# Three of four MLP batches by a seven-product scheme with weight sums kept in DRAM

## The chip, the cores and the metric

The kernel runs on one core of one Trainium2 chip. The metric is the device time of one execution in microseconds (us). Before the change three runs took 1020.67, 1022.09 and 1023.76 us; the median is 1022.09 us.

The core has a matrix engine (TensorE, PE in the profile; its weight loads are listed as PEld), a vector engine (VectorE, DVE), a scalar engine (ScalarE, ACT), GpSimd (POOL), and SyncE (SP), which here only issues DMAs. Matmuls write to PSUM, a memory of eight banks of 128 x 512 float32; GpSimd works on SBUF, the main on-chip memory. Each engine works through its own queue in order. A DMA waits, on the queue that issues it, for what it needs.

## What is computed

```python
def _attn_ref(q, k, v, centroids):          # B, H, S, D = 4, 8, 768, 64
    # q and k rows are assigned to one of 16 clusters each; a query sees the keys of its own cluster
    ...
    attn = softmax(where(mask, scale * q @ k.T, -1e9))
    return attn @ v

def _moe_ref(x, U, V, w_ch1, w_ch2):        # x: 4 x 768 x 512, w_ch1: 512 x 2048, w_ch2: 2048 x 512
    h = x.transpose(0, 2, 1) @ U @ V        # rank 32
    u = x + h.transpose(0, 2, 1)
    ch = np.maximum(u @ w_ch1, 0.0) @ w_ch2
    return u + ch
```

The change is in the last two lines, the MLP: two products with a ReLU between them, in four batches of 768 rows. All is float32.

## The kernel before

**Precision.** The MLP's products are done in a reduced 32-bit matmul type (F32R). A float32 value is therefore split into a high part (ScalarE copies it to F32R) and a low part (VectorE or GpSimd subtracts the high part). A product is three matmuls: high x high, high x low, low x high.

**Weights.** w1 and w2 arrive as the bits of 64-bit numbers, in four groups g of 512 hidden columns, each in 8 pieces of 128 x 512 (4 of w1, 4 of w2). `load_weights` takes a piece through six stages: a DMA (L151), ScalarE (`upper`, L159), three VectorE steps on integers (`join`, L171 to L183), and the split: ScalarE copies the high part (L204), GpSimd or VectorE subtracts (L205). The result stays in SBUF as `wg[g]` = w1h, w1l, w2h, w2l. Groups 0 and 1 are ready before the MLP begins, groups 2 and 3 are still being joined during its first half batch.

**The MLP.** There are eight half batches i of 384 rows. `fetch_u` reads the rows from DRAM, `turn_u` transposes them on PE (12 transposes) and splits them. Then come 16 steps f, one for each 128 hidden columns: `gemm1` (L606 to L608) makes 12 matmuls of 384 columns into one bank, ScalarE takes the ReLU as hh (L611), VectorE the low part hl (L612); `gemm2` (L622 to L624) uses hh and hl as stationary operands in 9 matmuls of 512 columns, which accumulate in three banks over all 16 steps. `gemm2` of step f comes after `gemm1` of step f + 1. `finish` adds u (L630) and stores 128 x 512 blocks.

**The order of work** is a list of events with planned times in units of one step f. The MLP begins at M0, half batch i at M0 + 16 i. The list is sorted by time, and each engine's instructions are fixed in that order; the times themselves are only a sort key. What runs late on an engine delays all that stands behind it there.

Of the kernel before, what the change touches and what calls it, by code (L numbers as in the profile page):

```python
# [52 lines left out]
FG = NF // NG  # L53
# [64 lines left out]
def clustered_attention_moe(ctx: ExitStack, tc: tile.TileContext, qk, v, cen, moe_U, moe_V, w1, w2, out):  # L118
# [68 lines left out]
    parts, pool = {}, {}  # L187
# [33 lines left out]
    def in_arena(at, k, n):  # L221
        return arena[:, at:at + k * n].rearrange("p (k n) -> p k n", k=k)
# [101 lines left out]
    n = B * NP  # L324
    NS = 2 * NT
    NG4 = 4 * NT
    live = {}
# [237 lines left out]
            nc.sync.dma_start(out=u_scr[b], in_=x)  # L565


    nh = 2 * B

    free = 2 * XS + 4 * 2048  # L570
    turned = {0: [in_arena(free, ND, HS), in_arena(free + ND * HS, ND, HS)]}

    def open_mlp():

        early.close()
        sb = pool["sb"] = ctx.enter_context(tc.tile_pool(name="msb", bufs=1, reuse_waits="tile"))
        pool["y"] = ctx.enter_context(tc.tile_pool(name="ps_y", bufs=4, space=PSUM, reuse_waits="tile"))
        wg[2].append(weight_tile(2, "w2l", sb))
        turned[1] = [sb.tile([P, ND, HS], F32R, name=name) for name in ("uh", "ul")]

    def open_weights():
        tail.close()
        right = ctx.enter_context(tc.tile_pool(name="wpool3", bufs=1, side="right", reuse_waits="tile"))
        wg[3] = [weight_tile(3, name, right) for name in names]

    def fetch_u(i):
# [13 lines left out]
    def gemm1(i, f):  # L600
        w1h, w1l, _, _ = wg[f // FG]
        uh, ul = turned[i % 2]
        fs = slice((f % FG) * P, (f % FG) * P + P)
        ps = work("ps_h")
        for d in range(ND):
            nc.tensor.matmul(ps[:, 0:HS], w1h[:, d, fs], uh[:, d, :], start=(d == 0), stop=False)  # L606
            nc.tensor.matmul(ps[:, 0:HS], w1h[:, d, fs], ul[:, d, :], start=False, stop=False)  # L607
            nc.tensor.matmul(ps[:, 0:HS], w1l[:, d, fs], uh[:, d, :], start=False, stop=(d == ND - 1))  # L608
        hh = pool["sb"].tile([P, HS], F32R, name="hh", bufs=3)
        hl = pool["sb"].tile([P, HS], F32R, name="hl", bufs=3)  # L610
        nc.scalar.activation(hh, ps[:, 0:HS], AF.Relu)  # L611
        nc.vector.scalar_tensor_tensor(out=hl, in0=ps[:, 0:HS], scalar=0.0, in1=hh, op0=ALU.max, op1=ALU.subtract)  # L612
        live["h", i, f] = hh, hl
# [12 lines left out]
    def finish(i):  # L626
        b, h = divmod(i, 2)
        u, y = live.pop(("u", i)), live.pop(("y", i))
        for t in range(HT):
            nc.vector.tensor_add(u[:, t, :], y[t], u[:, t, :])  # L630
            nc.sync.dma_start(out=out[b, (h * HT + t) * P:(h * HT + t + 1) * P, :], in_=u[:, t, :])

# [35 lines left out]
    for i in range(n):  # L668
# [24 lines left out]
        for k in range(NS):  # L693
            h, c = divmod(k, NT)
# [10 lines left out]
    for b, (t_u, t_sum, t_v) in enumerate(zip(*mixes.values())):  # L705
        o = NS * (NP * b + NP - 1)
# [58 lines left out]
```

## Time and profile before

| | |
|---|---|
| runs | 1020.67, 1022.09, 1023.76 us |
| profiled execution: span from first to last instruction | 1018.5 us |
| its own time beside the span | not given; the median of the runs is 3.6 us above the span |
| MLP: first gemm1 matmul to the last gemm2 matmul | 463.1 to 1014.2 us |
| one steady half batch | 68.3 us |
| granted PE clock in the MLP | 1.00 |

The profile is one execution. A group row gives the line of the code, the engine, the operation, output and inputs, shape and count, then the sum of busy time and the mean length, then the idle time before it and what ended it. In an order-of-time view the first number is the start, the second the length. A busy PE need not be at its peak: matmuls are pipelined, so the distance from start to start is their price, and it is shorter than the length shown.

### The profile page before, as it was taken

The page shows a single profiled execution, that of the slowest core. Times are in us where ns is not written, and L with a number is a line of the kernel's source. Part 1 is how long each engine was busy: PE and PEld are TensorE (multiplying, and loading weights), DVE is VectorE, ACT ScalarE, POOL GpSimd, SP SyncE. Part 2 cuts the span into 40 slices and gives each one's busy share as a digit, 9 for nine tenths or more (in the row PEclk, how much of TensorE's full clock was granted, in tenths as well). Part 3 has the DMA queues.
Part 4 walks back from the last instruction along what each step waited for, and adds up shares of the span by engine and source line. Part 5 has one row for each costly group of instructions (what it writes and reads, how often), then busy time and mean ns, then how long its engine had stood idle before and what let it go on. Part 6 is the DMA issues. An engine that isn't in the chain of part 4 may idle for free.

```text
span 1018.5 us, 13723 instructions
## 1 busy us (share of the span) xinstructions
PE 990.5 (97%) x5368; PEld 786.9 (77%) x5368; DVE 490.5 (48%) x914; ACT 347.7 (34%) x572; POOL 359.4 (35%) x246
## 2 busy tenths in 40 slices
PE   5899999999999999989999999999999999999998
PEld 3566666676667666657899999999999999998997
DVE  5797777777777666768772121121221211212211
ACT  4454554555556554564341111111111111111110
POOL 5466676888788967753230000000000000000000
PEclk9899999999999999999999999999999999999999
DMA  7754554656465636243431001010010010100000
GB/s 186 191 130 115 157 146 122 192 155 156 100 199 136 150 86 181 61 143 108 163 123 63 1 32 32 1 62 1 1 63 1 18 46 1 62 1 1 32 1 32
DMA packets 28687, 87.71 MB, mean 86 GB/s; under 512 B 4880, under 2 KB 9488, under 8 KB 28112
## 3 DMA queue, kind: packets, MB, share of 16 engines
q1 hardware_dynamic: 28240, 86.76, 30.5%
q8 instruction: 42, 0.69, 0.3%
q14 instruction: 21, 0.17, 0.1%
q10 hardware_dynamic: 384, 0.10, 0.0%
HBM read 42.99 MB, written 12.58 MB: 55 GB/s over the span
## 4 chain that ended last, share of the span: by engine, by line
PE 90%; DVE 5%; ACT 1%; issue 1%; POOL 1%; DMA 1%; ACTq 0%; SPq 0%; POOLq 0%; DVEq 0%
PE o_ps L500 12%; PE ps_h L606 9%; PE ps_h L608 9%; PE ps_h L607 9%; PE y L624 9%; PE y L623 9%; PE y L622 9%; PE ps_max L453 7%; PE st L477 6%; PE st L479 6%; DVE m L455 2%; PE ps_sum L512 1%; PE ps_sim L343 1%; PE ps_oT L533 1%; PE ps_uT L595 1%
## 5 line engine op out<-in xcount | busy, mean ns | idle before, releaser
L492 POOL TENSOR_TENSOR T<-T,pr 128x768 f32<-128x768 f32 x120 | 226.5, 1887 | 44.9 <-ACT pr L482 19.3
L612 DVE SCALAR_TENSOR_TENSOR hl<-ps_h,hh 128x384 fp32r<-128x384 f32 x128 | 71.2, 556 | 349.9 <-ACT hh L611 349.8
L455 DVE TENSOR_REDUCE m<-ps_max 128x1 f32<-128x384 f32 x384 | 195.2, 547 | 80.6 <-PE ps_max L453 79.0
L611 ACT ACTIVATE hh<-ps_h 128x384 fp32r<-128x384 f32 x128 | 62.9, 491 | 373.8 <-PE ps_h L608 373.8
L482 ACT ACTIVATE pr<-st 128x768 f32<-128x768 f32 x192 | 154.3, 812 | 83.5 <-PE st L479 65.4
L453 PE MATMUL ps_max<-arena 128*128 128x384 f32 x384 | 126.6, 380 | 6.9 <-DVE oh L369 2.5
L500 PE MATMUL o_ps<-pr,vt 128*64 128x384 f32 x768 | 132.2, 494 | 0.1
L623 PE MATMUL y<-w2l,hh 128*128 128x512 f32 x288 | 113.6, 395 | 0.0
L477 PE MATMUL st<-arena 128*128 128x384 f32 x384 | 104.9, 354 | 2.0 <-ACT pr L482 2.0
L453 PEld LDWEIGHTS ps_max<-arena 128*128 128x128 f32 x384 | 70.5, 192 | 45.4 <-issue 21.4
L500 PEld LDWEIGHTS o_ps<-pr,vt 128*64 128x64 f32 x768 | 52.7, 138 | 66.4 <-issue 59.8
L479 PE MATMUL st<-arena 97*128 97x384 f32 x384 | 99.2, 340 | 2.8 <-DMA arena<-mT 2.8
L477 PEld LDWEIGHTS st<-arena 128*128 128x128 f32 x384 | 66.2, 190 | 17.9 <-issue 9.3
L492 POOL TENSOR_TENSOR T<-pr 128x768 f32<-128x768 f32 x30 | 56.6, 1886 | 62.2 <-ACT pr L482 62.2
L624 PE MATMUL y<-w2h,hl 128*128 128x512 f32 x192 | 76.1, 396 | 0.0
L624 PE MATMUL y<-arena,hl 128*128 128x512 f32 x192 | 76.0, 396 | 0.0
L622 PE MATMUL y<-w2h,hh 128*128 128x512 f32 x192 | 75.1, 391 | 0.0
L622 PE MATMUL y<-arena,hh 128*128 128x512 f32 x192 | 74.8, 390 | 0.0
L479 PEld LDWEIGHTS st<-arena 97*128 97x128 f32 x384 | 70.4, 190 | 3.5 <-issue 2.2
L623 PEld LDWEIGHTS y<-w2l,hh 128*128 128x128 f32 x288 | 54.0, 188 | 9.1
L504 ACT COPY os<-o_ps 128x384 f32<-128x384 f32 x32 | 15.3, 480 | 104.7 <-PE o_ps L500 104.7
L606 PE MATMUL ps_h<-arena,w1h 128*128 128x384 f32 x128 | 44.8, 350 | 0.2 <-DVE arena L598 0.2
(132 smaller groups left out, 1597.3 us busy)
## 6 DMA issues: line engine op xcount, KB each, us to landing
rw<-in_w SPq DMA_DIRECT2D x32, 512.0 KB
R<-in_qk SPq DMA_DIRECT2D x32, 384.0 KB
arena<-arena SPq DMA_DIRECT2D x32, 384.0 KB
arena<-arena SPq DMA_DIRECT2D x64, 192.0 KB
vt<-in_v SPq DMA_DIRECT2D x16, 384.0 KB
u_scr<-xt SPq DMA_DIRECT2D x4, 1536.0 KB
u<-u_scr SPq DMA_DIRECT2D x8, 768.0 KB
out_y<-u SPq DMA_DIRECT2D x24, 256.0 KB
```

The source lines that it names most:

```text
L453: nc.tensor.matmul(ps[:, 0:HS], x1[:, 0, g // 2, g % 2, t * P:(t + 1) * P], x1[:, 1, h, g % 2, :], start=True, stop=True)
L455: nc.vector.reduce_max(live["m2", i][:, h, u:u + 1], ps[:, 0:HS], axis=AX.X)
L477: nc.tensor.matmul(st[:, j, 0:HS], x1[:, 1, hk, j, ks], x1[:, 0, h, j, :], start=True, stop=False)
L479: nc.tensor.matmul(st[:, j, 0:HS], x2[0:97, 1, hk, j, ks], x2[0:97, 0, h, j, :], start=False, stop=True)
L482: nc.scalar.activation(pr, st[:, :, 0:HS], AF.Exp, scale=SCALE)
L492: eng.tensor_add(T, live["p", i, h, 0] if c == 1 else T, live["p", i, h, c])
L500: nc.tensor.matmul(o_ps[64 * j:64 * j + 64, 0:HS], vv[:, c, j, :], pr[:, j, :], start=(c == 0), stop=(c == NT - 1))
L606: nc.tensor.matmul(ps[:, 0:HS], w1h[:, d, fs], uh[:, d, :], start=(d == 0), stop=False)
L607: nc.tensor.matmul(ps[:, 0:HS], w1h[:, d, fs], ul[:, d, :], start=False, stop=False)
L622: nc.tensor.matmul(y[t], hh[:, ts], w2h[:, f % FG, :], start=(f == 0), stop=False)
L623: nc.tensor.matmul(y[t], hh[:, ts], w2l[:, f % FG, :], start=False, stop=False)
L624: nc.tensor.matmul(y[t], hl[:, ts], w2h[:, f % FG, :], start=False, stop=(f == NF - 1))
```

## The change

Batch 0 (half batches i = 0 and 1, `nh = 2`) stays as it was. Batches 1 to 3 go another way: each product of a 2 x 2 block matrix is made by seven block products in place of eight (Strassen's scheme in Winograd's form).

**Sums of weights.** For each of the four groups and for w1 and w2, the four 256 x 256 blocks A11, A12, A21, A22 give four sums S1 to S4. This is done once, during batch 0: `recover` adds high and low parts (VectorE, 4 a step), `combine` makes the sums (GpSimd, 4), `split` splits them again (ScalarE copy, GpSimd subtract, then a DMA; 4, in two output buffers that take turns), `store_block` writes A11, A12, A22 (6 DMAs). Seven high and low blocks of a step, 3.67 MB, go to DRAM (`wc`); eight steps, one every 2.9 f-steps from M0 + 1 on.

**Batches 1 to 3.** `fetch_half` and `turn_half` bring in u as before, transposed; `u_sums` (VectorE) and `u_halves` (ScalarE, GpSimd) make its seven split blocks. A batch is 16 stretches of seven products: eight of the first matrix (`seven1`, K = 0 to 7) and eight of the second (`seven2`), in the order 1 1 1 2 1 2 1 2 1 2 1 2 1 2 2 2. A product is 6 matmuls of 384 columns with the weights stationary, into a PSUM bank of its own; the eight banks go round. So the output is transposed, and the host turns it back. `after1` adds the products up in SBUF (VectorE; ReLU on ScalarE), `h_sums` (VectorE) and `h_halves` (ScalarE, GpSimd) make the seven split blocks of the hidden layer, `after2` adds the second products to y and to four accumulators, `join_up` joins these after a batch; in the last batch `after2` does so itself in its last two stretches. The weights come from `wc` by `fetch_w1` and `fetch_w2`, two buffers deep, 29.4 MB a batch, all on SP's queue.

The rest moves buffers and reads w1 in another row order. The diff, cut:

```diff
+    wc = [[dram.tile([P, 2, 7, 512], F32, name=f"wc{k}_{g}") for g in range(NG)] for k in range(2)]
...
-    nh = 2 * B
+    nh = 2
...
+    def store_block(k, g, name, part):
+        nc.sync.dma_start(out=wc[k][g][:, :, slot[k][name], part * 256:part * 256 + 256],
+                          in_=blocks(k, g, part)[name].bitcast(F32))
+    def recover(k, g, j):
+        hi, lo = (blocks(k, g, part)[("A21", "A11", "A22", "A12")[j]] for part in range(2))
+        nc.vector.tensor_add(temps(k)[j], hi.bitcast(F32), lo.bitcast(F32))
+    def combine(k, j):
+        f = temps(k)
+        if j == 0:
+            nc.gpsimd.tensor_sub(f[1], f[0], f[1])
...
+    def split(k, g, j):
+        w = temps(k)[(1, 0, 2, 3)[j]]
+        o = pool["f"][:, 4096 + 1024 * (j % 2):5120 + 1024 * (j % 2)].rearrange("p (a n) -> p a n", a=2)
+        hi, lo = (o[:, :, part * 256:part * 256 + 256] for part in range(2))
+        nc.scalar.copy(hi.bitcast(F32R), w)
+        nc.gpsimd.tensor_sub(lo.bitcast(F32R), w, hi)
+        nc.sync.dma_start(out=wc[k][g][:, :, slot[k][("S3", "S1", "S2", "S4")[j]], :], in_=o)
...
+    def bank():
+        count["bank"] += 1
+        ps = work("ps_p") if count["bank"] % 2 else pool["y"].tile([P, 512], F32, name="ps_q", tag="y")
+        return ps[:, 0:HS]
...
+    def seven1(b, K, s):
+        ps = live["p", b, K, order[0][s]] = bank()
+        w = w1s[K % 2][:, 512 * s:512 * s + 512].rearrange("p (h k q) -> p h k q", h=2, k=2)
+        u = uc[order[0][s]]
+        for k in range(2):
+            nc.tensor.matmul(ps, w[:, 0, k], u[:, 0, k], start=(k == 0), stop=False)
+            nc.tensor.matmul(ps, w[:, 0, k], u[:, 1, k], start=False, stop=False)
+            nc.tensor.matmul(ps, w[:, 1, k], u[:, 0, k], start=False, stop=(k == 1))
...
+        elif key == T1:
+            h[B22] = ring()
+            add(h[B22], ps, h[B21])
+            add(h[B12], ps, h[B12])
+            nc.scalar.activation(h[B22], h[B22], AF.Relu)
...
+    def h_halves(b, K, key):
+        x = live["f", b, K][key]
+        out_ = live["h", b, K, key] = spare.pop(0)
+        hi, lo = out_[:, 0], out_[:, 1]
+        nc.scalar.copy(hi, x)
+        nc.gpsimd.tensor_sub(lo, x, hi)
...
+    def after2(b, m, e):
+        s, q = divmod(e, 2)
+        key = order[1][s]
+        ps = live.pop(("q", b, m, e))
+        y = pool["ys"][b % 2]
+        own = {B22: y[:, q, 1], B21: y[:, q, 0], T4: y[:, q + 2, 0]}.get(key)
+        if own is None:
+            own = pool["acc"][key][:, q]
+            if m == 0:
+                nc.scalar.copy(own, ps)
+                return
+        nc.vector.tensor_add(own, ps, own)
+        if b < B - 1 or m < NG - 1:
+            return
...
+    for k, (g, j) in enumerate((g, j) for g in range(NG) for j in range(2)):
+        c = M0 + 1 + 2.9 * k
+        for r in range(4):
+            at(c + 0.3 * r, recover, j, g, r)
+            at(c + 0.9 + 0.6 * r, combine, j, r)
+            at(c + 1.2 + 0.6 * r, split, j, g, r)
+        for r, name in enumerate(("A11", "A12", "A22")):
+            for half in range(2):
+                at(c + 0.4 * (2 * r + half), store_block, j, g, name, half)
...
+    U = 0.25
+    for b in range(1, B):
+        o = M0 + NF * nh + 28 * (b - 1)
...
+        seq = [(1, 0), (1, 1), (1, 2), (2, 0), (1, 3), (2, 1), (1, 4), (2, 2), (1, 5), (2, 3),
+               (1, 6), (2, 4), (1, 7), (2, 5), (2, 6), (2, 7)]
...
-        "in_w1": bits["w1"].reshape(ND, P, NG, FG * P).transpose(2, 1, 0, 3),
+        "in_w1": bits["w1"].reshape(ND, P, NG, FG, P).transpose(2, 1, 3, 0, 4).reshape(NG, P, FG, ND * P),
...
-    return r.results[0]["out_y"]
+    y = r.results[0]["out_y"].reshape(B, S, DM)
+    return np.concatenate([y[:1], y[1:].reshape(B - 1, DM, S).transpose(0, 2, 1)])
```

More of the change, by code (lines that the diff above doesn't have):

```diff
@@ new lines, in clustered_attention_moe, with blocks @@
+    order = ((B11, T2, T3, T1, B21, T4, B22), (B22, B11, B21, T1, T3, T2, T4))
+    slot = [{left[key]: s for s, key in enumerate(keys)} for keys in order]
+    def blocks(k, g, part):
+        x = wg[g][2 * k + part]
+        a12, a21 = (x[:, 0:2, 256:512], x[:, 2:4, 0:256])[::1 - 2 * k]
+        return {"A11": x[:, 0:2, 0:256], "A12": a12, "A21": a21, "A22": x[:, 2:4, 256:512]}
+    def store_block(k, g, name, part):
+        nc.sync.dma_start(out=wc[k][g][:, :, slot[k][name], part * 256:part * 256 + 256],
+                          in_=blocks(k, g, part)[name].bitcast(F32))
@@ new lines, in clustered_attention_moe, with pieces, pair, open_sevens @@
+    w1s = [w0.rearrange("p k i n -> p (k i n)")[:, 3584 * k:3584 * k + 3584] for k in range(2)]
+    spare, count = [], {"bank": 0, "f": 0}
+    def pieces(x, n):
+        return [x[:, k * n:(k + 1) * n] for k in range(x.shape[1] // n)]
+    def pair(x):
+        return x.rearrange("p (h n) -> p h n", h=2)
+    def open_sevens():
+        pool["w2s"] = [[arena[:, 0:3584]], [arena[:, 3584:6144], wg[2][3].rearrange("p i n -> p (i n)")[:, 0:1024]]]
+        pool["ys"] = [x.rearrange("p (d t n) -> p d t n", d=ND, t=2) for x in pieces(pool["f"], ND * S)]
+        at_end = w0.rearrange("p k i n -> p (k i n)")[:, 7168:7936]
+        spare.extend(pair(x) for x in (arena[:, 16896:17664], arena[:, 17664:18432], at_end,
+                                       wg[2][3].rearrange("p i n -> p (i n)")[:, 1024:1792]))
+        pool["st"] = rows.tile([P, HT, DM], F32, name="st", tag="R")
+        ring = []
+        for _ in range(2):
+            ring += pieces(raw.tile([P, 512], I64, name="rw").bitcast(F32)[:, 0:768], HS)
+        for _ in range(2):
+            ring.append(raw.tile([P, 512], F32, name="rw_g")[:, 0:HS])
+            ring.append(raw.tile([P, 512], I32, name="rw_t").bitcast(F32)[:, 0:HS])
+        pool["ring"] = ring
@@ new lines, in ring, with fetch_half, turn_half @@
+    def ring():
+        count["f"] += 1
+        return pool["ring"][count["f"] % len(pool["ring"])]
+    def bank():
+        count["bank"] += 1
+        ps = work("ps_p") if count["bank"] % 2 else pool["y"].tile([P, 512], F32, name="ps_q", tag="y")
+        return ps[:, 0:HS]
+    def fetch_half(b, h):
+        nc.sync.dma_start(out=pool["st"], in_=u_scr[b][:, h * HT:(h + 1) * HT, :])
+    def turn_half(b, h, d):
+        ps = work("ps_uT")[:, 0:HS] if b == 1 else bank()
+        for t in range(HT):
+            nc.tensor.transpose(ps[:, t * P:(t + 1) * P], pool["st"][:, t, d * P:(d + 1) * P], ident)
+        nc.scalar.copy(pool["ys"][b % 2][:, d, h], ps)
@@ new lines, in u_block, with u_sums @@
+    def u_block(b, key):
+        k, t = int(key[1]) - 1, int(key[2]) - 1
+        return pool["ys"][b % 2][:, 2 * k:2 * k + 2, t]
+    def u_sums(b, key):
+        live["t", key] = [ring() for _ in range(2)]
+        for k, to in enumerate(live["t", key]):
+            b11, b12, b21, b22 = (u_block(b, x)[:, k] for x in (B11, B12, B21, B22))
+            one, two = {T1: (b12, b11), T3: (b12, b22), T2: (b22, live["t", T1][k]),
+                        T4: (b21, live["t", T2][k] if key == T4 else None)}[key]
+            nc.vector.tensor_sub(to, one, two)
@@ new lines, in fetch_w2, with w2_slot @@
+    def fetch_w2(K, s0, s1):
+        g, a = divmod(K, 2)
+        at = 0
+        for x in pool["w2s"][K % 2]:
+            n = x.shape[1] // 512
+            lo, hi = max(s0, at), min(s1, at + n)
+            if lo < hi:
+                nc.sync.dma_start(out=x[:, 512 * (lo - at):512 * (hi - at)].bitcast(F32),
+                                  in_=wc[1][g][:, a, lo:hi].rearrange("p s n -> p (s n)"))
+            at += n
+    def w2_slot(K, s):
+        for x in pool["w2s"][K % 2]:
+            n = x.shape[1] // 512
+            if s < n:
+                return x[:, 512 * s:512 * s + 512]
+            s -= n
@@ new lines, in h_sums @@
+    def h_sums(b, K, key):
+        h = live["f", b, K]
+        one, two = {T1: (B12, B11), T3: (B12, B22), T2: (B22, T1), T4: (B21, T2)}[key]
+        h[key] = ring()
+        nc.vector.scalar_tensor_tensor(out=h[key], in0=h[one], scalar=0.0, in1=h[two], op0=ALU.max, op1=ALU.subtract)
+    def h_halves(b, K, key):
[4 more added lines that the diff above has]
+        nc.gpsimd.tensor_sub(lo, x, hi)
@@ new lines, in seven2 @@
+    def seven2(b, m, e):
+        s, q = divmod(e, 2)
+        key = order[1][s]
+        ps = live["q", b, m, e] = bank()
+        for j in range(2):
+            w = w2_slot(2 * m + j, s).rearrange("p (h q n) -> p h q n", h=2, q=2)[:, :, q]
+            h = live["h", b, 2 * m + j, key]
+            nc.tensor.matmul(ps, w[:, 0], h[:, 0], start=(j == 0), stop=False)
+            nc.tensor.matmul(ps, w[:, 0], h[:, 1], start=False, stop=False)
+            nc.tensor.matmul(ps, w[:, 1], h[:, 0], start=False, stop=(j == 1))
+            if q:
+                spare.append(live.pop(("h", b, 2 * m + j, key)))
@@ new lines, in twice @@
+    def twice(x, n):
+        return x.unsqueeze(1).broadcast_to([P, n, HS])
+    def after2(b, m, e):
+        s, q = divmod(e, 2)
+        key = order[1][s]
+        ps = live.pop(("q", b, m, e))
[9 more added lines that the diff above has]
+            return
+        if key == B11:
+            for t in range(2):
+                x = y[:, q:q + 3:2, t]
+                nc.gpsimd.tensor_add(x, x, twice(own, 2))
+        elif key == T1:
+            x = y[:, q:q + 3:2, 1]
+            nc.gpsimd.tensor_add(x, x, twice(own, 2))
+        elif key == T3:
+            nc.vector.tensor_add(y[:, q + 2], y[:, q + 2], twice(own, 2))
+        elif key == T2:
+            nc.vector.tensor_add(y[:, q, 1], y[:, q, 1], own)
+            store(b, q)
+            nc.vector.tensor_add(y[:, q + 2], y[:, q + 2], twice(own, 2))
+        elif key == T4:
+            store(b, q + 2)
```

153 lines of the change are left out of this document (140 added, 13 removed).

## The prediction

> **What bounds the kernel now.** I read the page's engine shares and its chain of waits first. TensorE is busy 97% of the span, and 90% of the chain that ended last is its own work.
>
> ```profile
> span 1018.5 us, 13723 instructions
> ...
> PE 990.5 (97%) x5368; PEld 786.9 (77%) x5368; DVE 490.5 (48%) x914; ACT 347.7 (34%) x572; POOL 359.4 (35%) x246
> ...
> PE 90%; DVE 5%; ACT 1%; issue 1%; POOL 1%; DMA 1%; ACTq 0%; SPq 0%; POOLq 0%; DVEq 0%
> ```
>
> Then the busy times by stretch: half a batch is one i of the MLP; the first two rows are i = 0, the third a steady one. Columns: length, then PE, PEld, DVE, ACT, POOL, granted clock, DMA share, GB/s.
>
> ```profile
> 463.00:500.00 37.00, 36.87 (x193) 30.80 (x194) 30.04 (x45) 15.65 (x30) 11.22 (x8) 1.00 0.43 135
> 500.00:536.00 36.00, 36.00 (x187) 32.29 (x186) 24.95 (x39) 14.03 (x28) 12.34 (x9) 1.00 0.41 133
> 604.40:673.00 68.60, 68.60 (x352) 62.04 (x351) 12.94 (x23) 9.79 (x20) 0.00 (x0) 1.00 0.07 24
> ```
>
> PE is full throughout at full clock. In steady halves the others are nearly idle; in i = 0 VectorE is busy 55 of 73 us. So the MLP lasts as long as its matmuls, and fewer columns are worth their time as long as PE stays fed. PE's order of time gives the prices (start, length):
>
> ```profile
> 599.45 0.49 PE L595 MATMUL ps_uT<-ident,u 128*128 128x128 f32 x3
> 667.73 0.49 PE L595 MATMUL ps_uT<-ident,u 128*128 128x128 f32 x3
> ...
> 612.33 0.33 PE L606 MATMUL ps_h<-arena,w1h 128*128 128x384 f32 x1
> ...
> 614.43 0.39 PE L622 MATMUL y<-w2h,hh 128*128 128x512 f32 x1
> ...
> 652.11 0.39 PE L622 MATMUL y<-arena,hh 128*128 128x512 f32 x1
> ...
> 654.20 0.49 PE L595 MATMUL ps_uT<-ident,u 128*128 128x128 f32 x3
> ```
>
> The same transposes return after 68.28 us: one half. Twelve 384-column matmuls take 614.43 - 612.33 = 2.10 us, 175 ns each; nine of 512 columns take 2.09 us, 232 ns each. Sixteen such steps are 67.0 us, so four groups of transposes take 1.24 us.
>
> **1. The seven products.** A batch now costs 136.56 us. After the change it has 8 x 7 x 6 = 336 matmuls of 384 columns for w1 and 4 x 14 x 6 = 336 for w2; 672 x 0.175 = 117.6 us, and the 24 transposes stay, 2.5 us: 120.1 us. Three batches save 3 x 16.5 = **49.4 us**. Nothing hides this, since PE sets the end. No row shows a long run of 384-column matmuls, only twelve at a time between longer ones. The weight loads bound it from above:
>
> ```profile
> L606 PEld LDWEIGHTS ps_h<-uh,w1h 128*128 128x128 f32 x112 | 21.1, 188 | 0.7
> ```
>
> If loads of 188 ns could not overlap, 2016 matmuls would take 13 ns more each, 26.2 us. I take 175: in the run of twelve it holds from the first to the last. The Trainium skill (Perfetto Trace Analysis, Identifying the Most-Contended Engine) judges TensorE by the busy share of its weight loads and not by its matmul share; by that, the steady half above stands at 90%, and an all-384 stream would want 107%, so that only 7.7 us a batch would be left to save.
>
> **2. Making the weight sums, during batch 0.** Eight steps (four weight groups, w1 and w2), one every 2.9 f-steps from f = 1, each with 4 adds on VectorE (recover), 4 adds and 4 subtracts on GpSimd (combine, split), 4 copies on ScalarE, 6 + 4 DMAs on SP's queue; all 128x512 or 256 KB and more. VectorE and GpSimd do not run side by side here:
>
> ```profile
> 467.09 1.29 POOL L205 TENSOR_TENSOR arena<-rw_t,arena 128x512 fp32r<-128x512 f32 x1 [2.47 <-ACT arena L204]
> 467.19 1.74 DVE L183 SCALAR_TENSOR_TENSOR rw_t<-rw,rw_t 128x512 int32<-128x512 int32 x1
> 471.28 0.42 DVE L178 TENSOR_SCALAR rw_t<-rw_g 128x512 int32<-128x512 int32 x1
> 471.35 1.49 POOL L205 TENSOR_TENSOR arena<-rw_t,arena 128x512 fp32r<-128x512 f32 x1 [2.97 <-ACT arena L204]
> ...
> 489.81 0.69 DVE L183 SCALAR_TENSOR_TENSOR rw_t<-rw,rw_t 128x512 int32<-128x512 int32 x1
> ```
>
> Alone L183 takes 0.69 us; begun during a GpSimd subtract it ends 0.55 us after that one's end (468.38 + 0.55 = 468.93). The subtract that met L178 ended 1.14 us after it (471.70 + 1.14). So an op on two SBUF operands and a GpSimd op take turns, at 0.55 and 1.15 us. Already in this stretch:
>
> ```profile
> L183 DVE SCALAR_TENSOR_TENSOR rw_t<-rw,rw_t 128x512 int32<-128x512 int32 x16 | 20.5, 1284 | 0.3
> L180 DVE SCALAR_TENSOR_TENSOR rw_t<-rw_g,rw_t 128x512 int32<-128x512 int32 x16 | 11.8, 745 | 0.3
> L178 DVE TENSOR_SCALAR rw_t<-rw_g 128x512 int32<-128x512 int32 x16 | 7.8, 490 | 8.8 <-ACT rw_g L159 8.8
> ```
>
> The new work comes on top while weight groups 2 and 3 are still being joined. From 470 us (the first combine) until the last w2l is ready there are 15 subtracts of weights and 38 new GpSimd ops (four steps whole, six of the fifth), 53 x 1.15 = 61 us; 20 recovers and 28 joins of two operands, 48 x 0.55 = 26 us; 14 shifts of 0.28 us, 4 us: 91 us in turns. The time that there is:
>
> ```profile
> 534.92 1.29 POOL L205 TENSOR_TENSOR w2l<-rw_t,w2h 128x512 fp32r<-128x512 f32 x1 [2.60 <-ACT w2h L204]
> ...
> 537.78 0.39 PE L622 MATMUL y<-w2h,hh 128*128 128x512 f32 x1
> ```
>
> PE needs that w2l at 537.78: 68 us. So about 23 us are missing, and all of it reaches PE: split has two output buffers, its ScalarE copy waits for the DMA store of two splits before, and behind that copy stand hh of gemm1, VectorE's hl and with them gemm2; VectorE's recover likewise stands ahead of hl. The other steps (26 GpSimd ops, 12 recovers, 36.5 us) have 8.8 f-steps of 4.19, 36.9 us: just enough. Bounds: GpSimd alone, 53 x 1.29 = 68 us, costs 0; turns with a tenth idle cost 33. I take **22 us**, near the turns, since each row that overlaps shows them.
>
> DMA in this stage: 29.4 MB of stores, 12.6 in rows of 1 KB and 16.8 of 2 KB, beside 8.4 MB of weights, some 6 MB of u and outputs, and 7.3 MB of first fetches.
>
> ```profile
> 507.00:508.00 1.00, 1.00 (x6) 0.86 (x6) 0.00 (x0) 0.00 (x0) 0.00 (x0) 1.00 1.10 467
> 1015.50:1016.50 1.00, 0.00 (x0) 0.00 (x0) 0.00 (x0) 0.00 (x0) 0.00 (x0) 1.00 1.02 377
> 15.50:16.00 0.50, 0.50 (x6) 0.00 (x0) 0.00 (x0) 0.50 (x1) 0.00 (x0) 1.00 0.89 197
> ```
>
> Weight loads run at up to 467 GB/s, output stores (2 KB rows) at 377, the rearrangement inside SBUF at 197. Rows of 1 KB to DRAM are not shown: at 377 GB/s the stage's DMA is 78 + 18 + 16 + 17 = 129 us, at 197 it is 159, against 137 us and the 22 of delay. I take 0, nearest the DRAM row; worst some 4 us, before the first product of batch 1, which waits in PE's order for its fetch.
>
> **3. Batches 1 to 3 beside PE.** The weight stream is 29.4 MB a batch, 245 GB/s over 120 us, below any DRAM row above: 0, with PE's next products as cover, two buffers deep; without that cover a fetch of 1.8 MB would cost 4 us and its landing. Its 35 or so issues a batch stand on SP's queue behind waits for PE and for the split stores alone, and nothing but PE's own products and the outputs waits behind them. The new row order of w1, the flat output and the later last gemm2 of i = 1 change no count of work: 0. The other engines' prices:
>
> ```profile
> L612 DVE SCALAR_TENSOR_TENSOR hl<-ps_h,hh x128: 543/557/559, 466.3 to 1011.0; 128x384 fp32r<-128x384 f32 x128
> L492 DVE TENSOR_TENSOR T<-pr x2: 945/948/950, 51.7 to 444.9; 128x768 f32<-128x768 f32 x2
> L492 POOL TENSOR_TENSOR T<-pr x30: 1853/1876/2184, 35.7 to 456.3; 128x768 f32<-128x768 f32 x30
> ```
>
> VectorE, per batch: 104 adds from PSUM x 0.557 = 58 us; 40 sums of 384 columns in SBUF at 0.56 (between 0.69 for 512 and 0.95 for 768, a line through both) = 22; 5 joins x 0.95 = 5: 85 us of 120. GpSimd: 56 subtracts at 1.01 (the same line) and 10 of 1.88: 75 us. ScalarE less. All fit, and eight PSUM banks give an add some 7 us of grace. Where three stretches of first products follow one another at a batch's start, GpSimd and the sums, in turns, want 3 x (7.1 + 4 x 0.42) us and the joins 10 more, in 22 us; the lag can pass the grace: I take **5 us** in all, between 0 and the 30 of a rival below.
>
> **4. The end.**
>
> ```profile
> 1013.25 2.09 DVE L630 TENSOR_TENSOR u<-y,u 128x512 f32<-128x512 f32 x3 [1.73 <-PE y L624]
> 1013.97 1.73 SPq L631 DMA_DIRECT2D out_y<-u  x3
> ...
> 1014.21 0.40 PE L624 MATMUL y<-w2h,hl 128*128 128x512 f32 x1
> ```
>
> Now the span ends 4.3 us after the last matmul starts. In the last batch's two final stretches GpSimd has six adds of 1.88, and VectorE behind them four of 768 columns, two of 384 and the last two sums: by these prices VectorE ends 6.6 us after PE, then 3 us of store: **+5 us** (3 to 8).
>
> **Sum.** On the profiled execution: 1018.5 - 49.4 + 22 + 5 + 5 = 1001.1 us of span. The profile gives no time beside the span; the median of the runs, 1022.1, is 3.6 us above it, which I leave: **1004.7 us**. Changes under 0.3% (3.1 us) this kernel can't tell from none.
>
> **Rivals.** *The sums of weights are covered* (part 2 costs 3, part 3 nothing): 1022.1 - 49.4 + 3 + 5 = 980.7. For it: GpSimd's own sum fits. Against: the turns. *Weight loads set PE's pace*, 188 ns: 1004.7 + 26.2 = 1030.9, slower than before; it decides from 183.6 ns (17.4 / 2016 more). For it: loads busy 90%. Against: 175 ns twelve times running. *VectorE becomes the bound of batches 1 to 3*: its 45 two-operand ops each wait out a GpSimd subtract, 85 + 45 x 1.0 = 130 us a batch, 30 in all in place of 5: 1029.7, slower; it sets the pace from 0.78 us of mean wait and is slower than before from 0.94. For it: the turns. Against: GpSimd is busy 63%, so a mean wait near 0.3. *The gain is eaten whole*: parts 2 and 3 together 45 us, within 0.3%.
>
> **Chances.** Forecast 0.56 (its own range 990 to 1018, part 2 from 8 to 33), covered 0.22, weight loads 0.08, VectorE 0.08, eaten 0.06. Faster 0.78; same 0.07, with a bit of the forecast's edge; slower 0.15. The range runs from the covered case less 3 us to just short of the two slow ones, 978 to 1028.
>
> **What would show it.** New matmul lines at 175 ns from start to start; a batch at 120 us; in the first 75 to 95 us of the MLP PE idle some 20 us, behind hh or hl, with GpSimd over 80% busy and recovers over 1 us; in batches 1 to 3 VectorE near 75%, DMA near 245 GB/s; some 10 us from the last matmul to the end. I am wrong if PE is as full in batch 0 as now, or if products wait for banks or fetches in every stretch.

## The result and the profile after

The changed kernel takes 1040.88 us (median; 1039.37 to 1041.96) against 1022.06 us (1020.67 to 1023.76): a ratio of 1.0181, 95% interval 1.0165 to 1.0196. It is slower; 1004.7 us had been forecast, and the time lies outside the range. The profiled execution has a span 20.8 us longer than before.

The page after: TensorE (PE) has as many matmuls as before, but its share of the chain that ended last fell from 90% to 65%.

```profile
span 1039.3 us, 15374 instructions
...
PE 963.8 (93%) x5368; PEld 787.4 (76%) x5368; DVE 758.2 (73%) x1256; ACT 474.5 (46%) x829; POOL 719.5 (69%) x523
...
PE 65%; DVE 11%; POOL 10%; issue 5%; DMA 4%; ACT 3%; DVEq 0%; SPq 0%; ACTq 0%; POOLq 0%
```

PE's order of time after (start, length): the first matmul of each half of batch 0, the first product, two products one stretch of 42 matmuls apart, and the last.

```profile
463.88 0.44 PE L612 MATMUL ps_h<-arena,w 128*128 128x384 f32 x1 [0.22 <-DVE arena L604]
...
565.39 0.34 PE L612 MATMUL ps_h<-u,w 128*128 128x384 f32 x1
...
652.26 0.34 PE L794 MATMUL ps_p<-arena,w 128*128 128x384 f32 x1
...
661.30 0.33 PE L795 MATMUL ps_p<-arena,w 128*128 128x384 f32 x1
...
668.58 0.33 PE L795 MATMUL ps_q<-arena,w 128*128 128x384 f32 x1
...
1028.01 0.34 PE L850 MATMUL ps_q<-h,w2l 128*128 128x384 f32 x1
```

The same marks before are 463.13, 535.69, 603.97 and 1014.21; the two in the middle:

```profile
535.69 0.34 PE L606 MATMUL ps_h<-uh,w1h 128*128 128x384 f32 x1
...
603.97 0.34 PE L606 MATMUL ps_h<-arena,w1h 128*128 128x384 f32 x1
```

So:

| | before | after | difference |
|---|---|---|---|
| up to the MLP | 463.1 | 463.9 | +0.8 |
| batch 0, first half | 72.6 | 101.5 | +28.9 |
| batch 0, second half | 68.3 | 86.9 | +18.6 |
| batches 1 to 3 | 410.2 | 375.8 | -34.5 |
| last matmul to the end | 4.3 | 11.3 | +7.0 |

The products run as forecast: 7.28 us for 42 matmuls, 173.3 ns each. All of the loss is around them. The stretches after (columns as in the forecast: length, PE, PEld, DVE, ACT, POOL, granted clock, DMA share, GB/s):

```profile
464.00:500.00 36.00, 31.30 (x162) 24.70 (x162) 34.43 (x39) 14.98 (x28) 24.86 (x17) 1.00 0.67 210
500.00:540.00 40.00, 31.09 (x127) 26.66 (x128) 31.31 (x40) 13.70 (x25) 29.81 (x22) 0.87 0.86 303
540.00:565.40 25.40, 18.13 (x90) 14.76 (x89) 22.58 (x25) 9.87 (x20) 21.87 (x15) 1.00 0.80 260
565.40:600.00 34.60, 31.03 (x141) 27.19 (x139) 15.48 (x20) 8.92 (x17) 27.07 (x20) 0.90 0.79 275
600.00:654.00 54.00, 47.49 (x232) 41.87 (x231) 16.15 (x23) 17.02 (x35) 28.70 (x22) 0.94 0.67 242
654.40:770.00 115.60, 113.21 (x651) 111.88 (x650) 88.74 (x136) 55.20 (x114) 74.46 (x64) 0.99 0.70 250
```

In the first half (three rows) PE is busy 80.5 of 101.4 us and VectorE 88.3; in the second VectorE is busy 31.6 of 88.6, and yet PE stands 10 us. So the two halves have different limits. What PE waits for in the first (engine, tile and line, by whom; total, times, longest):

```profile
PE y L629 <- DVE hx L617: 7.4, 5, 2.7
PE y L628 <- POOL w2l L205: 4.6, 3, 2.1
PE ps_h L612 <- DVE hx L617: 4.1, 2, 3.2
```

More than half of the 20.9 us that PE stands (11.5) is for hl, which VectorE writes (L617). What VectorE does ahead of it, groups of the first half, after:

```profile
L183 DVE SCALAR_TENSOR_TENSOR rw_t<-rw,rw_t 128x512 int32<-128x512 int32 x16 | 20.2, 1261 | 0.2
L180 DVE SCALAR_TENSOR_TENSOR rw_t<-rw_g,rw_t 128x512 int32<-128x512 int32 x16 | 17.9, 1123 | 0.2
L662 DVE TENSOR_TENSOR f<-arena 128x512 f32<-128x512 f32 x12 | 14.5, 1223 | 0.0
L178 DVE TENSOR_SCALAR rw_t<-rw_g 128x512 int32<-128x512 int32 x16 | 13.1, 816 | 9.8 <-ACT rw_g L159 9.2 <-POOL w2l L205 0.6
L662 DVE TENSOR_TENSOR f<-w 128x512 f32<-128x512 f32 x8 | 10.6, 1334 | 0.0
```

The joins of weights took 40.1 us before and take 51.2; 20 recovers (L662) add 25.1. The shortest recover took 0.63 us, so some 13 of the 36 us added are work (20 x 0.63), and the other 23 or so are VectorE waiting for its turn with GpSimd.

The second half: what ScalarE waits for there.

```profile
ACT f L679 <- DMA wc<-f: 10.5, 2, 6.9
ACT f L679 <- POOL f L673: 9.3, 3, 3.8
ACT f L679 <- POOL f L667: 8.4, 3, 3.0
...
ACT f L679 <- POOL f L671: 7.6, 3, 2.7
ACT f L679 <- POOL f L669: 6.1, 3, 2.3
```

ScalarE stands 41.9 us ahead of the split's copy (L679), behind GpSimd's combines (L667 to L673) and behind the stores that empty the split's two buffers, with everything that comes later on ScalarE behind it. One of these waits is the one that PE feels most. ScalarE's and PE's order of time there:

```profile
620.62 0.62 ACT L679 CAST f<-f 128x512 fp32r<-128x512 f32 x1 [6.89 <-DMA wc<-f]
621.14 0.47 ACT L740 COPY f<-ps_uT 128x384 f32<-128x384 f32 x1
...
621.66 0.90 PE L739 MATMUL ps_uT<-ident,st 128*128 128x128 f32 x3 [4.68 <-ACT f L740]
```

The last sum's copy stands 6.89 us for a store, the copy of u (L740) comes behind it, and PE's transposes of u (L739) stand 4.68 us for that; then the granted clock is 0.54 from 621 to 627.5 us. Step by step against before, PE loses 11.8 us between steps 9 and 12 of this half, most of it here. Another 6.3 us it loses in the first two steps, where it stands for the last pieces of weights (1.48 us for w2h, 1.63 for w2l), which the first half left late.

### The profile page after: what moved, and what is told of

It reads as the page before. It is cut to its first block, busy times and chain, and to the rows that moved or that the text cites. A ratio compares the mean times of both kernels' runs of the same rounds, so it can differ in the third digit from the quotient of the medians.

```text
span 1039.3 us, 15374 instructions
## 1 busy us (share of the span) xinstructions
PE 963.8 (93%) x5368; PEld 787.4 (76%) x5368; DVE 758.2 (73%) x1256; ACT 474.5 (46%) x829; POOL 719.5 (69%) x523
## 4 chain that ended last, share of the span: by engine, by line
PE 65%; DVE 11%; POOL 10%; issue 5%; DMA 4%; ACT 3%; DVEq 0%; SPq 0%; ACTq 0%; POOLq 0%
PE o_ps L502 11%; PE ps_max L455 7%; PE st L479 6%; PE st L481 5%; POOL f L680 3%; PE ps_p L794 2%; PE ps_p L796 2%; PE ps_p L795 2%; PE ps_q L848 2%; PE ps_q L850 2%; PE ps_q L849 2%; PE ps_q L796 2%; PE ps_q L794 2%; PE ps_q L795 2%; DMA wc<-f 2%
## 5 line engine op out<-in xcount | busy, mean ns | idle before, releaser
L457 DVE TENSOR_REDUCE m<-ps_max 128x1 f32<-128x384 f32 x384 | 195.3, 549 | 80.8 <-PE ps_max L455 79.2
L680 POOL TENSOR_TENSOR f<-f 128x512 fp32r<-128x512 f32 x32 | 43.1, 1347 | 30.8 <-ACT f L679 30.8
L794 PE MATMUL ps_p<-arena,w 128*128 128x384 f32 x178 | 59.9, 336 | 1.1 <-DVE f L869 0.7
L795 PE MATMUL ps_p<-arena,w 128*128 128x384 f32 x178 | 59.5, 334 | 0.0
L796 PE MATMUL ps_p<-arena,w 128*128 128x384 f32 x178 | 59.5, 334 | 0.0
L617 DVE SCALAR_TENSOR_TENSOR hx<-ps_h,hx 128x384 fp32r<-128x384 f32 x32 | 17.7, 553 | 56.4 <-ACT hx L616 56.3
L794 PE MATMUL ps_q<-arena,w 128*128 128x384 f32 x158 | 53.5, 339 | 0.0
L796 PE MATMUL ps_q<-arena,w 128*128 128x384 f32 x158 | 52.8, 334 | 0.0
L795 PE MATMUL ps_q<-arena,w 128*128 128x384 f32 x158 | 52.8, 334 | 0.0
L679 ACT CAST f<-f 128x512 fp32r<-128x512 f32 x32 | 19.8, 620 | 69.3 <-POOL f L673 16.0
```

Source lines behind the costliest of these rows:

```text
L457: nc.vector.reduce_max(live["m2", i][:, h, u:u + 1], ps[:, 0:HS], axis=AX.X)
L680: nc.gpsimd.tensor_sub(lo.bitcast(F32R), w, hi)
L794: nc.tensor.matmul(ps, w[:, 0, k], u[:, 0, k], start=(k == 0), stop=False)
L795: nc.tensor.matmul(ps, w[:, 0, k], u[:, 1, k], start=False, stop=False)
L796: nc.tensor.matmul(ps, w[:, 1, k], u[:, 0, k], start=False, stop=(k == 1))
```

## The experiments

Batch 0's halves are read from PE's order of time in each run, from the first gemm1 matmul of a half to that of the next, and to the first product. Medians without an interval in the text below are of a single execution.

| run | first half | second half | span | runs' median |
|---|---|---|---|---|
| before | 72.6 | 68.3 | 1018.5 | 1022.06 |
| after | 101.5 | 86.9 | 1039.3 | 1040.88 |
| stores only | 79.2 | 77.1 | 1007.8 | 1009.56 |
| few stores | 100.0 | 78.7 | 1030.7 | 1032.98 |
| combine ahead | 102.6 | 81.3 | 1033.0 | 1035.01 |
| no store wait | 100.5 | 79.0 | 1029.6 | 1031.38 |
| both waits away | 101.0 | 76.7 | 1029.6 | 1031.86 |
| both waits, recovers out | 93.9 | 74.4 | 1019.9 | 1021.72 |
| recovers out | 96.9 | 84.9 | 1033.1 | 1035.85 |
| subtractions out | 92.3 | 82.2 | 1024.8 | 1026.80 |
| subtractions, combines out | 90.3 | 75.8 | 1016.4 | 1017.93 |
| these and store wait out | 86.0 | 78.1 | 1015.2 | 1015.19 |

**Stores only.** Recover, combine and the split's computation are gone; every byte is still stored, from the weights.

```diff
-        nc.scalar.copy(hi.bitcast(F32R), w)
-        nc.gpsimd.tensor_sub(lo.bitcast(F32R), w, hi)
-        nc.sync.dma_start(out=wc[k][g][...], in_=o)
+        nc.sync.dma_start(out=wc[k][g][...], in_=wg[g][2 * k][:, 0:2, :].bitcast(F32))
...
-            at(c + 0.3 * r, recover, j, g, r)
-            at(c + 0.9 + 0.6 * r, combine, j, r)
```

> The sums of weights are left out (no recover, combine and split on VectorE, GpSimd and ScalarE); all DMA stores stay, with unsummed weights in the places of S1 to S4, so batches 1 to 3 multiply by wrong weights, with the same work. Theory 'engines' (GpSimd, VectorE and ScalarE set batch 0's pace): batch 0, 191 us after the change and 141 before, comes back to 141 to 148 us, and the time falls to about 990 to 998. Rival 'DMA' (88 MB of traffic more, 29 MB of it in batch 0, holds it up): batch 0 stays above 170 us and the time above 1018.

1009.56 us, between the two: the sums' work on the engines costs 31 us, but the stores are not free. In the second half PE stands 4.9 us for u, which is fetched behind them and behind the first weights of the products, all on SP's queue:

```profile
PE ps_uT L738 <- DMA st<-u_scr: 4.9, 1, 4.9
```

**Few stores.** All engine work stays; only group 0's blocks are stored, and the fetches read those.

```diff
+        if g == 0:
             nc.sync.dma_start(out=wc[k][g][...], in_=o)
```

> All of the sums' work on the engines stays; only group 0's sums are stored (7.3 of 29.4 MB) and all fetches read group 0's, so the results of batches 1 to 3 are wrong. Theory 'engines set the first half, DMA a part of the second': first half 96 to 102 us (the 6.6 us that it took longer with stores alone come on top of the engines' or lie under them), second half of batch 0 (86.9 after, 77.1 with stores alone) 70 to 77; time 1024 to 1033. Rival 'DMA': first half below 85, time below 1015.

1032.98 us; the whole and the first half are as expected, the second half, 78.7, is above its 70 to 77. In the first half the engines alone cost 27.4 of 28.9 us and the stores lie beside them. In the second the engines alone cost 10.4 and the stores alone 8.8, which comes near 18.6, but these are not its two parts: with the whole change PE does not wait for u's fetch at all, where the stores alone cost it most.

**Combine ahead, and no store wait.** The first puts each combine before the split of the sum before, so that GpSimd need not finish it just in time. The second lets the split's store read the weights, so that its buffers are free at once.

```diff
-            at(c + 0.9 + 0.6 * r, combine, j, r)
+            at(c + (0.9, 1.1, 1.7, 2.3)[r], combine, j, r)
```

> One change of order: each step's combine r + 1 stands ahead of split r on GpSimd, so that GpSimd adds while ScalarE copies. Theory 'handing over' (GpSimd stands idle 0.7 to 1.0 us before each of the 32 split subtracts, 30.8 us of idle time in the profile, because its next op waits for ScalarE's copy of what it has just made): this idle time falls below 10 us, batch 0 becomes 15 to 28 us shorter, time 1012 to 1026. Rival 'turns alone' (VectorE and GpSimd taking turns on two-operand work is the whole cost): no more than 5 us, since the work in turns is the same. Rival 'DMA': no change.

```diff
-        nc.sync.dma_start(out=wc[k][g][...], in_=o)
+        nc.sync.dma_start(out=wc[k][g][...], in_=wg[g][2 * k][:, 0:2, :].bitcast(F32))
```

> All work of the sums and all bytes of the stores stay, but split's store reads unsummed weights in place of the output buffer, so ScalarE's copy never waits for a store (the stored sums are wrong). Theory 'handing over' puts 15 us of ScalarE's waits down to these stores, of which the part ahead of hh reaches PE: batch 0 shorter by 5 to 15 us, time 1026 to 1036. If the two output buffers are what sets the pace: 30 us or more, below 1012. If they cost nothing: 1039 to 1042.

1035.01 (outside its range; GpSimd's idle time ahead of its subtractions fell from 30.8 to 20.5 us and not below 10) and 1031.38 us (inside). Neither moves the first half. The second becomes 5.6 and 7.9 us shorter, although ScalarE's standing ahead of L679 only falls from 41.9 to 38.9 and 37.3 us. With the combine ahead most of it has another releaser, the stores:

```profile
ACT f L679 <- DMA wc<-f: 29.8, 9, 8.4
ACT f L679 <- POOL f L667: 9.1, 3, 3.4
```

**Recovers out.** 24 of the 32 recovers are left out (`if g == 0:` before the event).

> VectorE's recover is left out of the last six of the eight steps of sums (24 of 32 adds; the sums of groups 1 to 3 are then of old values and wrong), everything else stays. In the first half of batch 0 (101.5 us after the change, 72.6 before, 79 with no sums but all stores) twelve of the recovers meet GpSimd's work. Theory 'turns': each takes GpSimd's place for 0.55 us and stands ahead of hl for up to 1.7; the first half falls to 86 to 94 us, time 1021 to 1031. Rival 'GpSimd's own queue' (53 ops of 1.3 us and their hand-overs set the pace whatever VectorE does): the first half stays above 97 us, time above 1034.

1035.85 us; the first half lost only 4.6 us, near the rival. Taking VectorE's new work away is not enough: its joins still took 49.4 us in place of 40.1, in turns with GpSimd.

**Subtractions out; subtractions and combines out.**

```diff
-        nc.gpsimd.tensor_sub(lo.bitcast(F32R), w, hi)
+        nc.scalar.copy(lo.bitcast(F32R), w)
```

> Left out: the subtraction of every split (line 680), 32 of GpSimd's operations, in whose place ScalarE copies the sum a second time; recovers, combines and all stores stay, so the low parts that batches 1 to 3 use are not those of the reference. Theory 'GpSimd's queue and its hand-overs': in the first half of batch 0 (101.5 us with the change, 72.6 before, 79.2 with the stores alone) GpSimd is busy 76 us and stands some 14 us more behind ScalarE's copy; some 21 subtractions at 1.36 us and that standing leave the queue, so it no longer bounds anything and the first half takes 81 to 87 us; the whole 1018 to 1026 us. Rival 'turns': half of the operations that VectorE has to take turns with stay, so the half gains 5 to 9 us (93 to 97) and the whole comes to 1030 to 1036.

> Left out: the subtractions of the splits, as in the run before, and the combines (line 667), so that GpSimd has no work of the weight sums at all; VectorE's 32 recovers, ScalarE's copies and all stores stay. The sums stored are not those of the reference. Both theories: the first half of batch 0 falls to 79 to 83 us (79.2 with the stores alone), and the whole to 1010 to 1018 us. What it tells: if the run before is already there, the subtraction and its hand-over are the whole cost; if the step between the two is large, every GpSimd operation counts alike. If the half stays above 86 us, recovers and copies cost by themselves, which the run without most recovers spoke against.

1026.80 us (ratio 1.0046, 1.003 to 1.0062) and 1017.93 us (0.9961, 0.9945 to 0.9976). In the first run the first half fell by 9.2 us, just past the rival's 5 to 9; the whole came out between the two ranges, because the second half gained 4.7 too. Without both it stayed at 90.3 us, above the bound of 86 that had been set for 'recovers and copies cost by themselves'; ScalarE's 32 copies more may be part of that, which no run shows. VectorE's groups of the first half in the latter run:

```profile
L180 DVE SCALAR_TENSOR_TENSOR rw_t<-rw_g,rw_t 128x512 int32<-128x512 int32 x16 | 12.1, 763 | 0.2
L662 DVE TENSOR_TENSOR f<-arena 128x512 f32<-128x512 f32 x12 | 10.2, 864 | 0.0
...
L178 DVE TENSOR_SCALAR rw_t<-rw_g 128x512 int32<-128x512 int32 x16 | 8.5, 534 | 12.4 <-ACT rw_g L159 10.0 <-POOL w2l L205 2.4
```

The same operations on the same data: 763 for 1123 ns, 864 for 1223, 534 for 816. GpSimd's sums alone made them longer. The joins and the same 20 recovers take 53.0 us here in place of 76.3, so the 23 us of waiting for turns are gone with those sums.

**Both waits away.** Still open was whether ScalarE's standing ahead of L679, which the runs with the combine ahead and without the store's wait had mostly handed on to the other releaser, was what held the first half.

> Both at once: the combine a step ahead of the split, and the splits' stores read the weights in place of the sum's buffer (the stored sums are therefore not the reference's; all engine operations and all bytes stay). ScalarE stood 27 us ahead of the split's copy in the first half with the change, 18 with the combine ahead alone, 28 with the store's wait out alone. Theory 'a line behind a wait': without both releasers it stands under 8 us there, the first half takes 86 to 94 us and the whole 1016 to 1027 us, more than the two single runs together (5.8 and 9.5 us). Rival 'the operations themselves and their turns': the first half stays at 97 us or more, and the whole at 1026 to 1033.

1031.86 us, ratio 1.0092 (1.0062 to 1.0121). In the first half ScalarE's wait ahead of L679 fell from 27.4 to 11.5 us, and its length stayed (101.0): the rival holds there. In the second it fell to 12.5 us, and the half to 76.7 us:

```profile
ACT f L679 <- POOL f L667: 6.1, 3, 3.8
ACT f L679 <- POOL f L671: 3.8, 3, 1.9
ACT f L679 <- POOL f L673: 2.6, 2, 1.9
```

That is about the length with the stores alone (77.1), and as there PE now stands for u's fetch (2.9 us). So the theory of the line behind a wait falls for the first half and stands for the second, where taking both waits away gives back 10.2 of 18.6 us.

**And recovers out; or the sums out.** The first is the run just above without 24 recovers as well. The second leaves out the store's wait, the subtractions and the combines; the recovers stay.

> As the run before, and 24 of VectorE's 32 recovers left out. 'A line behind a wait': recovers were slow to matter while ScalarE held the line, so this takes 2 to 5 us more off the first half: 83 to 90 us. 'The operations themselves': 4.6 us as alone, so 92 to 96 us.

> Combines and subtractions left out, and the stores read the weights: recovers, ScalarE's two copies for each split and all bytes stay. The run with combines and subtractions out had 90.3 us in the first half and ScalarE standing 9.8 us behind the stores. 'A line behind a wait': 79 to 84 us, and the whole 1003 to 1011. 'The operations themselves': 86 to 90, and the whole 1013 or more.

1021.72 us (ratio 1.0000, 0.9983 to 1.0016) and 1015.19 (0.9928, 0.9903 to 0.9952), with 93.9 and 86.0 us in the first half: both as 'the operations themselves' had them, the second at the very edge. Without the waits the recovers are worth 7.1 us in place of 4.6, and with GpSimd's sums gone the store's wait is still worth 4.3 (90.3 against 86.0), so waits are not free in this half once the sums no longer fill it.

**Joins out.** At the borders of batches after, four pairs of stretches take 17.8 us more than 7.28 each. In this run `join_up` does not add, and the sums of u are spread (`sums + 0.5 * k`, `0.75 + 0.65 * k`).

> Batch boundaries: join_up's eight adds are left out (results of batches 1 and 2 wrong), and u_sums and u_halves keep their work but are spread over 4.5 steps in place of 3. Theory 'banks' (VectorE's adds of two SBUF operands wait for GpSimd, so PSUM banks come free late, and PE's pauses halve its clock): the stretches (2,0) of batches 2 and 3, 11.78 and 9.72 + 1.0 us now, fall to 7.3 to 8.3; the stretches (2,6) with (2,7) of batches 1 and 2, 19.1 us, fall to 15 to 17; together 9 to 13 us, time 1028 to 1032. Rival 'fetches' (w2 slots land late there): both keep their lengths, time 1039 to 1042.

1024.26 us, 4 us below the range: of the 17.8 us 15.7 came back, where 9 to 13 had been expected. PE's waits at the end of batch 1, after, show why so little waiting costs so much:

```profile
765.86 0.44 PE L848 MATMUL ps_q<-arena 128*128 128x384 f32 x1 [1.15 <-DVE acc L869]
768.42 0.69 PE L848 MATMUL ps_p<-h,arena 128*128 128x384 f32 x1 [1.24 <-DVE f L869]
```

Only 2.4 us of waits in a pair of stretches that is 4.6 us late; but the second matmul is 0.69 us long for 0.34, and the granted clock is 0.57 and 0.58 in the two stretches of 2 us from 768 us on. What VectorE does ahead of the add (L869) that ends the second wait:

```profile
766.53 1.37 DVE L753 TENSOR_TENSOR ring<-f,rw_g 128x384 f32<-128x384 f32 x1
767.82 0.55 DVE L869 TENSOR_TENSOR f<-ps_p,f 128x384 f32<-128x384 f32 x1
```

That is a sum of u (L753) for the next batch, and no join. The two ends of batches, 9.2 us of the 17.8, are of this kind. The two starts, 8.7 us, are where the joins (L902) stand on VectorE, with the sums of h (L831), ahead of the add at L809 that PE waits for:

```profile
805.93 0.69 PE L848 MATMUL ps_q<-arena 128*128 128x384 f32 x1 [2.08 <-DVE rw L809]
```

This run changed both at once and so does not part them; the run with two batches spread, below, does.

**Two batches.** If crowding is the cause and not the work, the same sums over two batches must be nearly free. Batches 0 and 1 go the old way; the sums begin at step 14, behind the joins of weights, one every 5.4 steps; batches 2 and 3 use seven products.

```diff
-    nh = 2
+    nh = 4
...
-        c = M0 + 1 + 2.9 * k
+        c = M0 + 14 + 5.4 * k
```

> Batches 0 and 1 as before, only 2 and 3 by seven products; the sums begin at step 14, after the last weight group's joins, one every 5.4 steps in place of 2.9. Theory 'engines': a step of sums needs about 16 us and now has 22.6, so batches 0 and 1 take what they took, and the time is 1022 - 33 + 7 for the tail + about 9 of stalls in two batches = 1005, faster than before. If DMA stores or their waits cost by themselves, not by crowding: about 1025 to 1040.

1008.34 us, 3 us above what was worked out, ratio 0.9864 (0.9848 to 0.9881): faster than before. The four halves take 72.7, 69.0, 68.3 and 73.9 us: all sums and stores cost 6.3 us (283.7 against 277.4) in place of 47.5.

**Two batches, spread.** To it come the combine ahead, the first fetches of w1 behind u's, joins every 1.2 steps, the sums of u spread, and half of the last batch's adds of B11 on VectorE.

> The version with two batches by seven products (1008.3 us), with GpSimd's combine ahead, the first two w1 fetches behind the u fetch, join_up and u_halves spread, and half of the last batch's first adds moved from GpSimd to VectorE. By the theories 'banks' and 'turns': 4 us at the hand-over (wait for u 2.5 and half clock), 6 to 8 us at the one boundary, 3 at the tail less: 994 to 999 us. If boundaries are set by fetches: 1003 to 1007.

1000.59 us (0.979, 0.9774 to 0.9807), 1.6 us above the range. The end of the first batch by seven products takes 15.6 us for its two stretches, in place of 19.2 in the run just above, with all joins still made: that excess was the sums of u. At the start, one stretch of the last batch took 12.22 us. VectorE's order of time there, and PE's:

```profile
894.88 1.13 DVE L831 SCALAR_TENSOR_TENSOR rw_t<-rw,ring 128x384 f32<-128x384 f32 x1
895.93 1.76 DVE L902 TENSOR_TENSOR f<-f,acc 128x768 f32<-128x768 f32 x1
897.62 1.35 DVE L831 SCALAR_TENSOR_TENSOR rw_g<-rw,rw_g 128x384 f32<-128x384 f32 x1
898.89 0.55 DVE L869 TENSOR_TENSOR f<-ps_q,f 128x384 f32<-128x384 f32 x1
```

```profile
897.57 0.34 PE L796 MATMUL ps_p<-arena,w 128*128 128x384 f32 x1
899.49 0.44 PE L794 MATMUL ps_q<-arena,w 128*128 128x384 f32 x1 [1.58 <-DVE f L869]
...
902.05 0.69 PE L794 MATMUL ps_p<-arena,w 128*128 128x384 f32 x1 [1.24 <-DVE f L869]
```

A join (L902) and two sums of h (L831), each in turns with GpSimd, stand ahead of the add (L869) that frees PE's next bank.

**Joins apart.** The joins go where VectorE has little else.

```diff
-                at(o + 28.6 + 1.2 * j, join_up, b, j)
+                at(o + 28 + (0.3, 1.0, 2.6, 6.0, 6.4, 6.6, 6.9, 7.3)[j], join_up, b, j)
```

> Computes all. As the two-batch version with the joins spread (1000.59 us), with the joins set not at even steps but where VectorE has little else: six of eight between steps 2.6 and 7.3 of the next batch, the last five of them from step 6.0 on, in and behind the stretch of second products. Theory 'a join on VectorE in the steps of the sums of h holds the next bank': the stretch of 12.22 us falls to 7.3 to 8.5, the whole to 995 to 998 us. Rival 'VectorE is short of time there wherever the joins stand': the excess moves to other stretches, 999 us or more.

996.09 us, ratio 0.9751 (0.9734 to 0.9767), as expected, and the fastest of all. Its two batches by stretch:

```profile
742.90:865.50 122.60, 122.23 (x706) 120.91 (x705) 92.90 (x146) 55.95 (x116) 81.34 (x70) 1.00 0.68 243
865.50:982.30 116.80, 116.80 (x673) 116.80 (x672) 97.87 (x142) 46.32 (x96) 81.15 (x64) 1.00 0.60 221
```

In this execution, the fastest of its four (993.32 us), PE is full at full clock. Against the run before only the moment of the eight joins was changed; five of them are VectorE's.

**Three batches, the same remedies.**

> Computes all, for three batches as the change does it: the combine one step ahead of the split, the sums of u spread, the joins where the run before has them, half of the last batch's joins of B11 on VectorE. Theory 'two costs that are apart': 5.8 us as in the run with the combine ahead, 12 to 17 us at the two borders of batches (their stretches are 17.8 us over 7.28 each), 0 to 1 at the end: 1017 to 1024 us, so no better than before in earnest, since batch 0 still holds 45 us more than before. Rival 'the borders cost wherever the joins stand': 1031 or more.

1025.54 us (1.0044, 1.0025 to 1.0063), 1.5 us above the range and not faster than before. The borders lost nearly all their excess, but u's fetch for the last batch now stood on SP's queue behind the joins' stores (PE stood 3.7 us for it), and batch 0 stayed at 101.8 and 82.6 us.

## Why the prediction was wrong, step by step

**The seven products: right.** 173.3 ns where 175 was taken. The rival of the weight loads is refuted by the row above with loads busy 116.80 of 116.80 us and matmuls on their pace: a load is 188 ns long there too, so one load overlaps the next, and 173 is what 232 ns for 512 columns come to for 384 (174). Refuted too, as a forecast of what could be saved here, is the busy share of the loads, which the Trainium skill (Perfetto Trace Analysis, Identifying the Most-Contended Engine) names as a measure of TensorE beside its share of peak arithmetic: loads at 100% took nothing from the saving.

**The sums of weights, first half: right in place and kind, short in size.** Forecast 22 us, within 0 to 33; measured 28.9, of which 27.4 come with hardly any stores. Turns were the reason given, and the runs show them: the first halves with VectorE's recovers out (-4.6), GpSimd's subtractions out (-9.2) and both of its parts out (-11.2) each give a part back, and removing waits alone, with all sums in place, gives nothing. Of the two paths to PE that were named, the one through ScalarE's copy is thereby not borne out; the other, hl late behind VectorE's work, is what PE's waits show (11.5 of 20.9 us). What the sum left out is the clock: 0.87 in the stretch from 500 to 540 us, 5 us in these 40. Of the 36 us by which VectorE's joins and recovers grew, some 13 are work and 23 turns, which are gone without GpSimd's sums. What share of the half's own length each of the two makes no run separates. The Trainium skill (SBUF — State Buffer, Who interferes with whom) has the turns as an exclusive lock between a VectorE operation with two SBUF inputs and GpSimd, and the lengthened L180 (1123 for 763 ns) and L662 (1223 for 864) agree; it names tensor_scalar among the operations that can take the shared port too, and the shift L178 is lengthened as well, 816 for 534 ns.

**The sums, second half: the step that failed.** "26 GpSimd ops, 12 recovers, 36.5 us [...] have 8.8 f-steps of 4.19, 36.9 us: just enough", so 0, and the DMA of the stage 0, at worst 4. Measured: 18.6 us. The comparison of work with time took for granted that GpSimd's next operation is always ready and that nothing of PE's stands in its chain. But a sum goes from GpSimd (combine) to ScalarE (copy), back to GpSimd (subtract) and to the DMA; ScalarE stood ahead of its copies, with PE's next operands behind it. The forecast had named this very wait, the store of two splits before, for the first half, and left it out of the second. When both releasers were taken away 10.2 us came back; one alone gave 5.6 or 7.9. The comparison also took the half to start on time, while the first half had left the last weights late: 6.3 of the 18.6 us arise in the first two steps. Of the 8.4 that remain without both waits, 2.5 lie there still, and most of the others behind u's fetch; with the stores alone it is 8.8, with PE standing for u and then at half clock (0.50 from 597 to 602 us). Bytes over bandwidth had shown no loss, because the total fitted; the one small fetch that PE needed did not.

**Batches 1 to 3: mis-sized, and half of it in another place.** Forecast 5 us, measured 17.8 at the borders of batches. Between the borders the forecast's view (near 75% and 245 GB/s) is right, with VectorE at 77% and 250 GB/s, and the rival that VectorE bounds every stretch is refuted. The lag was looked for at a batch's start, as a matter of work in 22 us. There, joins and sums of h on VectorE ahead of an add cost 8.7 us. The other 9.2 arise at a batch's end, which the forecast had left out: there the next batch's sums of u, in turns with GpSimd, stand ahead of the adds that free banks. In all PE stands some 10 us in these batches, and the lower clock behind the waits makes most of the difference to 17.8. With the sums of u spread and the joins apart, the same two places together cost 1.0 us in place of 8 to 10.

**The end**: +7.0 for +5, of the kind forecast, inside 3 to 8. The last adds:

```profile
1034.87 0.55 DVE L869 TENSOR_TENSOR f<-ps_q,f 128x384 f32<-128x384 f32 x1
```

VectorE ended 1035.42 - 1028.35 = 7.1 us after PE; 6.6 had been worked out.

**The rivals.** None of them was the course that it took. The slower time came from the sum of a term set to 0 (18.6), one within its bounds (6.9 over) and one mis-sized (12.8 over), 38.3 us together, where the span missed by 38.2; the end (2.0 over) and the quicker products (3.4 under) nearly cancel with what is left. The chance of 0.15 for slower rested on two mechanisms in the products alone; no rival gave batch 0 more than 33 us.

## What to carry to other kernels

Where work goes over several engines in turn, don't compare the sum of its operations with the time alone: follow one piece from engine to engine, and ask at each step what stands behind the waiting instruction; take releasers away together before judging, since one removed hands part of the wait to the next. And don't take the sum of a wait for its price: ScalarE's standing fell by a tenth while the half became 7.9 us shorter, because PE felt mainly one of fourteen waits. Work that is free over two batches can cost more than it saves when crowded into one. Before PE waits for VectorE, look at what small operation of no urgency stands ahead of the one that frees a bank, and move it.

## What the runs showed of the hardware

After two waits of PE of 1.58 and 1.24 us, with 1 us of matmuls between them, the granted clock was halved. Clock and rate of the run with two batches spread, by stretches of 2 us:

```profile
902.00:904.00 2.00, 1.95 (x6) 1.95 (x7) 1.48 (x3) 1.26 (x4) 2.00 (x3) 0.51 0.03 8
904.00:906.00 2.00, 2.00 (x10) 2.00 (x9) 1.52 (x3) 0.00 (x0) 1.13 (x1) 0.63 0.00 2
906.00:908.00 2.00, 2.00 (x13) 2.00 (x12) 1.58 (x3) 1.38 (x3) 0.21 (x1) 1.00 1.03 370
```

Some 3 us at 0.5: 2.8 us of waits cost 4.9 us of stretch. The Trainium skill (TensorE: Matmul & The Clock Gate, What's actually happening) has the clock fall after an idle window of about 3.4 us; here neither gap was that long, and the window was not idle throughout.
